# Transposed loads of k and v, the shift convolution on TensorE, and full-size first-stage tiles in an FFT convolution plus MLP kernel

## The chip, the cores and the metric

The kernel runs on one core of one Trainium2 chip. The metric is the device time of one execution in microseconds (us), the median of the fast runs. The kernel before takes 297.48 us (296.56 to 298.64, 4 runs). The profile's span is about 2 us shorter than that time: the span of the profiled run is 295.0 us.

Engines: PE is TensorE (PEld its weight loads), DVE is VectorE, ACT is ScalarE, POOL is GpSimd, SP is SyncE. Here SyncE issues every DMA, in one queue, in program order. "SPq" in the chain of waits is SyncE's own instruction stream.

## The reference

Two layers are applied twice to x, which starts as q (2048 rows of 512, bf16).

```python
# A: shift convolution, long convolution by FFT, gate
k_shift = sum over t of k_pad[:, t:t+S, :] * shift_k[:, 3 - t]     # 4 taps per channel
kv = k_shift * v
y = irfft(rfft(kv, zero padded to 2S) * rfft(ssm_k, padded)) [:S]  # long convolution
y = y + kv * ssm_D
x = x + layernorm(x) * y
# B: MLP
x = x + (gelu(layernorm(layernorm(x)) @ w1 + b1) @ w2 + b2)        # 512 -> 1376 -> 512
```

k, v, shift_k and ssm_k do not depend on x. So y is computed once, at the start, and everything after it is norms, gates and MLP blocks.

## The kernel before

A small list scheduler, `Prog`, takes operations with estimated durations and fixes the order on each engine. The program goes through these stages:

1. ssm_k (the filter) is loaded and transposed on TensorE, goes through a first transform stage (`stage1`) and a second (`stage2`, with a 6.3 MB table `tab_s2` that is loaded in 8 pieces). Result `R_H`.
2. k and v are loaded; VectorE makes the four taps of the shift convolution, adds them and multiplies with v (`shift_chunk`). Then `stage1`.
3. `products`: `stage2` of kv, times the filter's transform, on VectorE, in two halves.
4. Two inverse stages, then the norms of the first block.
5. Eight MLP blocks, four for each of the two passes.

The parts that the change touches:

```python
    dma(A(0, 128, R_SR, [1, 2048]), dr(A_shift_k, 0, [0, 128], [1, 2048]), 1 << 19)
    # ... two small loads of k for the rows that the taps reach back to ...
    for g in range(2):     # 64 partitions x 16 KB contiguous, 1 MB each
        dma(A(64 * g, 64, R_K + 1536, [1, 8192]), dr(A_k, 16 * g * 512, [32 * 512, 64], [1, 8192]), 1 << 20)
    for g in range(2):
        dma(A(64 * g, 64, R_V, [1, 8192]), dr(A_v, 16 * g * 512, [32 * 512, 64], [1, 8192]), 1 << 20)
    for j in range(8):     # the stage-2 table
        tload(t_s2, 64 * 384, j * 3072, R_S2 + j * 3072, 3072)
    # ... (cut)
    def shift_chunk(w):    # 7 operations of 128 x 2048 for each of 4 chunks
        # ... (cut: outputs tm)
        def tap(j, o):
            tt(o, A(0, 128, R_K + (3 - j) * 512 + w * 64, [512, 16], [256, 2], [1, 64]),
               A(0, 128, R_SJ[w] + j * 128, [0, 16], [64, 2], [1, 64]), ALU.mult, 1140.0)
        for j in range(3):
            tap(3 - j, tm[j])
        tt(tm[1], tm[0], tm[1], ALU.add, 1140.0)
        tap(0, tm[0])
        tt(tm[2], tm[1], tm[2], ALU.add, 1140.0)
        tt(tm[1], tm[2], tm[0], ALU.add, 1140.0)
        for h in range(2):
            # ... multiply with v, 128 x 1024 ...
        stage1(R_KP, ...)  # 512 matmuls in all, 64x64 weights, 128 columns; evicted by ScalarE alone
```

Of the kernel before, what the change touches and what calls it, by code (L numbers as in the profile page):

```python
# [44 lines left out]
class Prog:  # L45
# [7 lines left out]
    def __init__(self, nc):  # L53
        self.nc = nc
        self.ops = []
        self.state = {}
        self.nodes = [(-1, None)]
        self.cache = {}

# [60 lines left out]
    def op(self, eng, fn, dur, reads=(), writes=(), tile=None, dma=None, prio=0.0, nbytes=0, after=()):  # L120
# [4 lines left out]
        o.extra = prio  # L125
# [254 lines left out]
def _tables():  # L380
# [4 lines left out]
    F = np.stack([np.cos(th), -np.sin(th)], -1).reshape(64, 128)  # L385
    F = np.concatenate([F, F], 0)
# [25 lines left out]
AR = 105984  # L412


def bass_interleave_layers__ssm_conv_h3__mixer_channel_mlp__prompt_kernel(
# [3 lines left out]
    NS = 192  # L419
# [28 lines left out]
    R_ID, R_F, R_D, R_B1, R_SJ3 = place(128), place(128), place(16), place(16), place(512)  # L448
    R_S2 = place(64 * 384)
    R_1, R_2, R_3, R_4, R_5, R_6 = (place(n) for n in (16384, 16384, 17920, 16384, 8192, 5120))  # L450
# [4 lines left out]
    R_K, R_V, R_Y, R_U = R_3, R_3 + 19 * 512, R_3, R_3 + 16384  # L455
    R_GX, R_SR, R_X, R_T2 = R_4, R_4 + 12288, R_4, R_4 + 8192
    R_SJ = [R_4 + 8192 + 512 * w for w in range(3)] + [R_SJ3]
    R_KP, R_YT = R_5, R_5
    R_TMP, R_RING = R_6, R_6
    R_XT = R_S2  # L460
    R_HT = R_S2 + 4096
    R_N = R_S2 + 4096 + 2 * 5632
    M_B1, M_ST, M_MV, M_RS, M_HF = 0, 16, 16 + 96, 16 + 96 + 32, 16 + 96 + 32 + 16
# [15 lines left out]


    row = 128 + 128 + 512 + 4096
    P.op(ACT, lambda e: e.preload_act_table(AF.Gelu_apprx_tanh), 1300.0, prio=1e6)
    z = A(0, 1, R_K, [1, 1536])
    P.op(POOL, lambda e, z=z: e.memset(z, 0.0), 1300.0, writes=[z])
    tload(t_sm, row, 0, R_ID, 256)
    dma(A(0, 128, R_D, [1, 4]), dr(A_ssm_D, 0, [1, 128], [128, 4]), 1024)
    for b in range(4):
        dma(A(0, 128, R_HRAW + b * 2048, [1, 2048]), dr(A_ssm_k, b * 128 * 2048, [2048, 128], [1, 2048]), 1 << 19)
    dma(A(0, 128, R_SR, [1, 2048]), dr(A_shift_k, 0, [0, 128], [1, 2048]), 1 << 19)
    dma(A(64, 64, R_K, [1, 1536]), dr(A_k, 13 * 512, [32 * 512, 64], [1, 1536]), 3 << 16)  # L490
    dma(A(1, 63, R_K, [1, 1536]), dr(A_k, 29 * 512, [32 * 512, 63], [1, 1536]), 3 << 16)
    for g in range(2):
        dma(A(64 * g, 64, R_K + 1536, [1, 8192]), dr(A_k, 16 * g * 512, [32 * 512, 64], [1, 8192]), 1 << 20)
    for g in range(2):
        dma(A(64 * g, 64, R_V, [1, 8192]), dr(A_v, 16 * g * 512, [32 * 512, 64], [1, 8192]), 1 << 20)
# [3 lines left out]
    HP = 0.0  # L499
    EV_H = EV_X = (ACT,)  # L500
# [7 lines left out]
    for a4 in range(4):  # L508
        tl = Tile(dconv)
        for al in range(4):  # L510
            ins = []
            for b in range(4):
                for g in range(2):
                    src = A(0, 128, R_HRAW + b * 2048 + 16 * g + 4 * a4 + al, [32, 64])
                    ins.append((g, al * 512 + b * 128, src))

            def f(e, ins=ins, tl=tl):
                for g, o, src in ins:
                    r = e.transpose(QB(tl, 64 * g, 64, o, [1, 128]), src, IDN)
                return r  # L520
            P.op(PE, f, 8 * 60.0, reads=[x[2] for x in ins] + [IDN], tile=tl)
        dst = A(0, 128, R_HP + 16 * a4, [4, 4], [64, 128], [1, 4])

        def f(e, dst=dst, tl=tl):
            src = QB(tl, 0, 128, 0, [512, 4], [4, 128], [1, 4])
            if e is nc.scalar:
                return e.activation(dst, src, AF.Copy)
            return e.tensor_copy(dst, src)
        P.op((ACT, DVE), f, {ACT: 2048 * .833 + 60, DVE: 2048 * .52 + 70}, writes=[dst], tile=tl)

    def stage1(src, G, gk, gh, dg0, n, engs, prio=0.0):


        for d8 in range(dg0 // 8, (dg0 + n) // 8):
            for h in range(2):
                tl = Tile(dconv)
                ins = [(64 * g, i, A(64 * g, 64, src + (64 * h + 8 * d8 + i) * 64, [1, 64]), A(64 * g, 64, R_F, [1, 128]))
                       for i in range(8) for g in range(2)]

                def f(e, ins=ins, tl=tl):  # L540
                    for p, i, w, m in ins:
                        r = e.matmul(Q(tl, p, 64, i * 128, [1, 128]), w, m, start=True, stop=True)  # L542
                    return r
                P.op(PE, f, 16 * 45.0, reads=[x for y in ins for x in y[2:]], tile=tl, prio=prio)
                dst = A(0, 128, G + gh(h, 8 * d8), [gk, 128], [1, 8])

                def f(e, dst=dst, tl=tl):
                    src = Q(tl, 0, 128, 0, [1, 128], [128, 8])
                    if e is nc.scalar:
                        return e.activation(dst, src, AF.Copy)  # L550
                    return e.tensor_copy(dst, src)
                P.op(engs, f, {ACT: 1100.0, DVE: 1024 * 1.04 + 90}, writes=[dst], tile=tl, prio=prio)
# [19 lines left out]

    stage1(R_HP, R_GH, 128, lambda h, dg: 64 * (dg // 32) + 32 * h + dg % 32, 0, 64, EV_H, HP)
    for k4 in range(16):
        tl = stage2(R_GH, range(4 * k4, 4 * k4 + 4), 128, dconv, HP)
        dst = A(0, 128, R_H + k4 * 1024, [1, 1024])

        def f(e, dst=dst, tl=tl):
            src = Q(tl, 0, 128, 0, [1, 1024])
            if e is nc.scalar:  # L580
                return e.activation(dst, src, AF.Copy)  # L581
            return e.tensor_copy(dst, src)  # L582
        P.op((ACT, DVE), f, {ACT: 1024 * .833 + 60, DVE: 1024 * 1.04 + 70}, writes=[dst], tile=tl, prio=HP)

# [4 lines left out]
    for w in range(4):  # L589
        tt_out = A(0, 128, R_SJ[w], [128, 4], [64, 2], [1, 64])  # L590
        tt_in = A(0, 128, R_SR + 256 * w, [1, 4], [1024, 2], [4, 64])
        P.op(DVE, lambda e, o=tt_out, i=tt_in: e.tensor_copy(o, i), 600.0, reads=[tt_in], writes=[tt_out])

    def shift_chunk(w):

        tm = [A(0, 128, R_KP + w * 1024, [64, 16], [4096, 2], [1, 64])]
        tm += [A(0, 128, o, [128, 16], [64, 2], [1, 64]) for o in (R_TMP, R_TMP + 2048)]

        def tap(j, o):

            tt(o, A(0, 128, R_K + (3 - j) * 512 + w * 64, [512, 16], [256, 2], [1, 64]),
               A(0, 128, R_SJ[w] + j * 128, [0, 16], [64, 2], [1, 64]), ALU.mult, 1140.0)
        for j in range(3):
            tap(3 - j, tm[j])
        tt(tm[1], tm[0], tm[1], ALU.add, 1140.0)
        tap(0, tm[0])
        tt(tm[2], tm[1], tm[2], ALU.add, 1140.0)
        tt(tm[1], tm[2], tm[0], ALU.add, 1140.0)
        for h in range(2):
            tt(A(0, 128, R_KP + (64 * h + 16 * w) * 64, [4, 16], [64, 16], [1, 4]),  # L610
               A(0, 128, R_TMP + 64 * h, [128, 16], [4, 16], [1, 4]),
               A(0, 128, R_V + 256 * h + w * 64, [512, 16], [4, 16], [1, 4]), ALU.mult, 610.0)
        stage1(R_KP, R_GX + 8192 * (w // 2), 64, lambda h, dg: 32 * h + dg % 32, 16 * w, 16, EV_X)

    nx = [0]

    def products(hf):

        for k8 in range(8):
            tl = stage2(R_GX + 8192 * hf, range(8 * k8, 8 * k8 + 8), 64, dx)  # L620
            xo = R_RING + (nx[0] % 3) * 1024
            po = R_RING + 3072 + (nx[0] % 2) * 1024
            nx[0] += 1
            xb = A(0, 128, xo, [1, 1024])

            def f(e, xb=xb, tl=tl):
                return e.activation(xb, Q(tl, 0, 128, 0, [1, 1024]), AF.Copy)  # L627
            P.op(ACT, f, 1024 * .833 + 60, writes=[xb], tile=tl)
            ho = R_H + k8 * 2048 + 64 * hf
            x3 = A(0, 128, xo, [128, 8], [64, 2], [1, 64])  # L630
            tt(A(0, 128, po, [128, 8], [64, 2], [1, 64]), x3, A(0, 128, ho, [256, 8], [128, 2], [1, 64]), ALU.mult, 600.0)
            tt(x3, x3, A(0, 128, ho + 128, [256, 8], [-128, 2], [1, 64]), ALU.mult, 600.0)
            for ri, p in ((0, po), (1, xo)):
                tt(A(0, 128, R_Y + ri * 8192 + 8 * k8 * 64 + 32 * hf, [64, 8], [4096, 2], [1, 32]),
                   A(0, 128, p, [128, 8], [32, 2], [1, 32]), A(0, 128, p + 64, [128, 8], [32, 2], [1, 32]),
                   ALU.add if ri else ALU.subtract, 330.0)

    def inverse1(hf):

        for d4 in range(8 * hf, 8 * hf + 8):  # L640
            tl = Tile(dconv)
            ins = []
            for i in range(4):
                dg = 4 * d4 + i
                for ri in range(2):
                    ins.append((i, ri, A(0, 128, R_Y + ri * 8192 + dg, [64, 128]), A(0, 128, R_U + ri * 256, [1, 256])))
# [5 lines left out]
            P.op(PE, f, 8 * 115.0, reads=[x for y in ins for x in y[2:]], tile=tl)  # L652
            dst = A(0, 128, R_Z + 16 * d4, [256, 64], [4, 4], [1, 4])
# [206 lines left out]
```

## Time and profile before

What matters, with the stage borders read from the chain of waits and the timeline:

| stage (us) | before |
|---|---|
| start until v has landed and VectorE goes on | 35.7 |
| until the first product | 65.1 (+29.4) |
| until the first MLP matmul | 131.9 (+66.8) |
| until the end | 295.0 (+163.1) |

The span in 40 slices (7.4 us each) of the kernel before: a digit is the busy share in tenths, the last line what the DMA engines moved.

```profile
PE   0657086799899396329999999999999999999992
DVE  0135999999999998898890794874938611101131
DMA  6999997000099520003210301303003020200322
GB/s 203 297 213 213 224 414 284 2 18 6 2 224 296 197 97 2 1 5 69 51 20 2 71 0 28 46 0 63 8 2 71 18 53 2 71 0 2 71 71 71
```

The DMA engines are full in slices two to six, VectorE from the fifth to about the eighteenth, and TensorE from the nineteenth on. So three limits follow each other. The same with exact borders, from the busy times by window of the kernel before (columns: window, its length, then busy time of PE, PEld, DVE, ACT and POOL with instruction counts, granted clock, DMA share, GB/s):

```profile
0.00:35.70 35.70, 14.36 (x320) 12.81 (x320) 14.12 (x16) 14.20 (x13) 1.88 (x7) 0.95 0.94 224
35.70:65.10 29.40, 22.26 (x387) 18.98 (x388) 28.68 (x29) 22.57 (x24) 0.96 (x2) 0.83 0.51 196
65.10:131.90 66.80, 47.15 (x786) 41.95 (x785) 63.55 (x147) 46.65 (x52) 7.95 (x12) 0.87 0.33 92
131.90:295.00 163.10, 156.43 (x689) 64.32 (x702) 83.02 (x214) 59.54 (x88) 13.32 (x22) 0.98 0.17 36
```

VectorE is busy for 28.68 of the 29.4 us in which the shift convolution ends, and for 63.55 of the next 66.8. In the last stage it is TensorE, 156.43 of 163.1. The chain of waits of the kernel before (start, length, what) has the load of v as its first long piece:

```profile
7.51 28.18 DMA ar<-in_A_v_dram
35.69 4.62 DVE ar L587 x5
...
61.70 1.03 ACT ar L581
63.88 1.22 DVE ar L582
65.10 1.88 DVE ar L587 x4
```

The chain names v, but VectorE didn't stand still for it: by its timeline it had worked on k's taps without a gap since 25.4 us, and used v first at 36.7. So 35.7 is a border between stages, and no wait of the kernel before.

And the groups by shape (busy us, mean ns, idle time before them with its releaser). The 28 operations of 128x2048 are the shift convolution; of the 40 of 128x1024, 8 multiply with v and 32 are products.

```profile
L587 DVE TENSOR_TENSOR ar<-ar 128x2048 bf16<-128x2048 bf16 x28 | 32.9, 1220 | 7.3 <-DMA ar<-in_A_k_dram 7.0
L587 DVE TENSOR_TENSOR ar<-ar 128x1024 bf16<-128x1024 bf16 x40 | 25.9, 683 | 0.2
L542 PE MATMUL ps<-ar 64*64 64x128 bf16 x512 | 21.6, 241 | 17.3 <-DVE ar L587 10.9 <-ACT ar L550 3.1 <-ACT ar L527 2.8
```

### The profile page before, as it was taken

How to read it: one execution, taken by the hardware profiler on the slowest of the kernel's cores; microseconds unless marked ns; L12 is line 12 of the kernel's file. 1: busy time of each engine (PE TensorE's matmuls, PEld its weight loads, DVE VectorE, ACT ScalarE, POOL GpSimd, SP SyncE). 2: the span in 40 equal slices, each digit the busy share in tenths (PEclk: the TensorE clock that was granted, in tenths of full speed). 3: DMA queues.
4: the chain of work that ended last, by engine and by line, in shares of the span. 5: the costliest groups of instructions: out<-in, count | busy, mean ns of one | idle time of the engine just before them, and what ended most of it. 6: DMA issues, size and time to landing. Idle time of an engine off the chain costs nothing.

```text
span 295.0 us, 5161 instructions
## 1 busy us (share of the span) xinstructions
PE 240.2 (81%) x2177; PEld 138.1 (47%) x2192; DVE 189.4 (64%) x401; ACT 143.0 (48%) x176; POOL 24.1 (8%) x43
## 2 busy tenths in 40 slices
PE   0657086799899396329999999999999999999992
PEld 0655075588799284113433434434433444434440
DVE  0135999999999998898890794874938611101131
ACT  1069079598968469616327045152366321464000
POOL 2000000100010022210210110111101100000000
PEclk9999658999999879758999999999999999999997
DMA  6999997000099520003210301303003020200322
GB/s 203 297 213 213 224 414 284 2 18 6 2 224 296 197 97 2 1 5 69 51 20 2 71 0 28 46 0 63 8 2 71 18 53 2 71 0 2 71 71 71
DMA packets 22703, 25.75 MB, mean 87 GB/s; under 512 B 17722, under 2 KB 19355, under 8 KB 22170
## 3 DMA queue, kind: packets, MB, share of 16 engines
q1 hardware_dynamic: 22682, 25.44, 33.0%
q8 instruction: 17, 0.28, 0.4%
q14 instruction: 4, 0.03, 0.0%
HBM read 19.66 MB, written 2.10 MB: 74 GB/s over the span
## 4 chain that ended last, share of the span: by engine, by line
PE 51%; DVE 24%; DMA 10%; ACT 7%; SPq 2%; issue 2%; POOL 2%
PE ps L818 24%; PE ps L800 23%; DVE ar L587 16%; DMA ar<-in_A_v_dram 10%; DVE sm L729 3%; ACT ar L581 2%; SPq L470 2%; ACT ar L658 2%; DVE ar L743 2%; PE ps L650 2%; ACT ar L550 2%; ACT ar L627 1%; POOL sm L737 1%; DVE ar L582 1%; PE ps L566 1%
## 5 line engine op out<-in xcount | busy, mean ns | idle before, releaser
L805 ACT ACTIVATE ar<-ps,sm 128x512 bf16<-128x512 f32 (+1 forms) x88 | 59.5, 686 | 82.3 <-PE ps L800 59.1
L587 DVE TENSOR_TENSOR ar<-ar 128x512 bf16<-128x512 bf16 (+2 forms) x164 | 91.5, 618 | 8.9 <-DMA ar<-in_A_k_dram 7.0
L800 PE MATMUL ps<-ar 128*128 128x512 bf16 (+1 forms) x342 | 81.7, 385 | 1.6 <-ACT ar L789 1.2
L818 PE MATMUL ps<-ar 128*128 128x512 bf16 (+1 forms) x347 | 78.1, 379 | 0.8 <-DVE ar L822 0.6
L822 DVE TENSOR_TENSOR ar<-ar,ps 128x512 bf16<-128x512 bf16 x32 | 21.2, 682 | 65.5 <-PE ps L818 65.5
L800 PEld LDWEIGHTS ps<-ar 128*128 128x128 bf16 (+1 forms) x352 | 30.8, 101 | 50.8 <-ACT ar L805 21.4
L818 PEld LDWEIGHTS ps<-ar 128*128 128x128 bf16 (+1 forms) x352 | 33.6, 98 | 43.4 <-ACT ar L805 2.9
L729 DVE BATCH_NORM_STATS2 sm<-ar 128x6 f32<-128x512 bf16 x64 | 41.4, 681 | 0.1
L550 ACT ACTIVATE ar<-ps 128x1024 bf16<-128x1024 f32 x32 | 30.0, 1050 | 12.7 <-PE ps L542 12.7
L542 PE MATMUL ps<-ar 64*64 64x128 bf16 x512 | 21.6, 241 | 17.3 <-DVE ar L587 10.9
L566 PE MATMUL ps<-ar 128*128 128x128 bf16 (+1 forms) x192 | 30.0, 239 | 2.3 <-ACT ar L550 1.5
L743 DVE TENSOR_SCALAR ar<-ar,sm 128x512 bf16<-128x512 bf16 x64 | 23.2, 406 | 11.4 <-POOL sm L737 10.3
L568 PE MATMUL ps<-ar 128*128 128x64 bf16 (+1 forms) x192 | 29.2, 202 | 0.0
L567 PE MATMUL ps<-ar 128*128 128x64 bf16 (+1 forms) x192 | 29.1, 201 | 0.0
L542 PEld LDWEIGHTS ps<-ar 64*64 64x64 bf16 x512 | 17.9, 121 | 20.9 <-issue 9.1
L650 PE MATMUL ps<-ar 128*128 128x256 bf16 x128 | 17.7, 301 | 5.5 <-DVE ar L587 5.2
L566 PEld LDWEIGHTS ps<-ar 128*128 128x128 bf16 x192 | 18.7, 98 | 4.3 <-ACT ar L550 2.1
L568 PEld LDWEIGHTS ps<-ar 128*128 128x128 bf16 x192 | 18.8, 98 | 0.7
L650 PEld LDWEIGHTS ps<-ar 128*128 128x128 bf16 x128 | 15.7, 175 | 7.0 <-DVE ar L587 5.5
L567 PEld LDWEIGHTS ps<-ar 128*128 128x128 bf16 x192 | 18.8, 98 | 0.0
L627 ACT ACTIVATE ar<-ps 128x1024 bf16<-128x1024 f32 x16 | 15.9, 1043 | 3.3 <-DVE ar L587 3.1
L658 ACT ACTIVATE ar<-ps 128x1024 bf16<-128x1024 f32 x14 | 13.7, 1042 | 7.9 <-PE ps L650 7.9
(27 smaller groups left out, 97.0 us busy)
## 6 DMA issues: line engine op xcount, KB each, us to landing
ar<-tab_s SPq DMA_DIRECT2D x8, 768.0 KB, 34.1
ar<-in_A_ssm_k_dram SPq DMA_DIRECT2D x4, 512.0 KB, 5.5
ar<-in_A_k_dram SPq DMA_DIRECT2D x2, 1024.0 KB, 16.3
ar<-in_A_v_dram SPq DMA_DIRECT2D x2, 1024.0 KB, 25.9
ar<-in_A_q_dram SPq DMA_DIRECT2D x2, 1024.0 KB, 10.5
out_dram<-ar SPq DMA_DIRECT2D x8, 256.0 KB, 3.1
ar<-in_B_w_dram SPq DMA_DIRECT2D x1, 1376.0 KB, 8.5
ar<-in_B_w_dram SPq DMA_DIRECT2D x1, 1280.0 KB, 6.1
```

The lines of the kernel that those rows point to most:

```text
L542: r = e.matmul(Q(tl, p, 64, i * 128, [1, 128]), w, m, start=True, stop=True)
L550: return e.activation(dst, src, AF.Copy)
L566: e.matmul(Q(tl, 0, 128, i * 2 * n, [1, 2 * n]), t[0], gg[0], start=True, stop=False)
L567: e.matmul(Q(tl, 0, 128, i * 2 * n, [1, n]), t[1], gg[1], start=False, stop=False)
L568: r = e.matmul(Q(tl, 0, 128, i * 2 * n + n, [1, n]), t[2], gg[2], start=False, stop=True)
L587: return P.op(eng, lambda e: e.tensor_tensor(o, a, b, op), dur, reads=[a, b], writes=[o])
L650: r = e.matmul(Q(tl, 0, 128, i * 256, [1, 256]), w, m, start=ri == 0, stop=ri == 1)
L729: P.op(DVE, lambda e, st=st, x=x: e.bn_stats(st, x), 600.0, reads=[x], writes=[st])
L743: P.op(DVE, lambda e: e.tensor_scalar(o, x, m, r, ALU.subtract, ALU.mult), 260.0, reads=[x, m, r], writes=[o])
L800: r = e.matmul(Q(tl, 0, rows, 0, [1, 512]), w, m, start=dk == 0, stop=dk == 3)
L805: P.op(ACT, lambda e, dst=dst, tl=tl, rows=rows, bias=bias: e.activation(dst, Q(tl, 0, rows, 0, [1, 512]), AF.Gelu_apprx_tanh, bias=bias), ...
L818: r = e.matmul(Q(tl, 0, 128, 0, [1, 512]), ins[fc][0], ins[fc][1], start=fc == 0, stop=fc == 10)
```

## The change

The intent is to take the shift convolution off VectorE, which is the limit between 36 and 132 us, and give it to TensorE, which has time there. A convolution along rows, per channel, becomes a matmul with a diagonal weight matrix once channels lie on partitions: four taps are four matmuls with the data shifted by one column, summed in PSUM. For that k and v must arrive transposed, which the DMA can do (the kernel before has 28 such transposes of 128 KB inside SBUF, which held SyncE 1.27 us each, the median); and kv must be transposed back (four more DMA transposes, inside SBUF). The first transform stage then works on full 128x128 weights (128 matmuls of 256 columns for 512 of 128), its evictions are shared by ScalarE and VectorE, and the products are 2048 wide instead of 1024. Further on, the residual operations are merged to 2048 and a scheduling priority (`BIAS`) holds back the MLP blocks' operations in the scheduler's order.

```diff
-    for g in range(2):
-        dma(A(64 * g, 64, R_K + 1536, [1, 8192]), dr(A_k, 16 * g * 512, [32 * 512, 64], [1, 8192]), 1 << 20)
-    for g in range(2):
-        dma(A(64 * g, 64, R_V, [1, 8192]), dr(A_v, 16 * g * 512, [32 * 512, 64], [1, 8192]), 1 << 20)
+    for b in (0, 2, 1, 3):          # 4 transposes of 2048 rows x 128 channels, 512 KB
+        dmat(A(0, 128, R_KT + b * 2064 + 16, [1, 2048]), dr(A_k, 128 * b, [512, 2048], [1, 128]), 1 << 19)
+    for a in range(32):             # 32 transposes of 64 rows (32 apart) x 512 channels, 64 KB
+        dmat(A(0, 128, R_VT + 64 * a, [2048, 4], [1, 64]), dr(A_v, 512 * a, [32 * 512, 64], [1, 512]), 1 << 16)
     for j in range(8):
         tload(t_s2, 64 * 384, j * 3072, R_S2 + j * 3072, 3072)
@@ shift_chunk is replaced by kv(q), for the halves q = 0, 1 @@
+                    ins = [(A(0, 128, R_DG + (4 * b + j) * 128, [1, 128]),
+                            A(0, 128, R_KT + b * 2064 + 16 + 1024 * u + 512 * n - j, [1, 512])) for j in range(4)]
+                    def f(e, ins=ins, tl=tl, n=n):
+                        for j, (w, m) in enumerate(ins):
+                            r = e.matmul(Q(tl, 0, 128, 512 * n, [1, 512]), w, m, start=j == 0, stop=j == 3)
+                        return r
+                o = A(0, 128, R_KVT + 8192 * q + 64 * h + 32 * u, [128, 32], [1, 32])
+                v = A(0, 128, R_VT + 2048 * b + 32 * u, [64, 32], [1, 32])
+                P.op(DVE, lambda e, o=o, v=v, tl=tl: e.tensor_tensor(o, Q(tl, 0, 128, 0, [1, 32], [32, 32]), v, ALU.mult),
+                     1225.0, reads=[v], writes=[o], tile=tl, prio=KP[q])
+        for i in range(2):          # kv back, SBUF to SBUF, 512 KB each
+            dmat(A(0, 128, R_KP + 4096 * q + 2048 * i, [128, 16], [1, 128]), A(0, 128, R_KVT + 8192 * q + 2048 * i, [1, 2048]), 1 << 19, ...)
+        stage1(R_KP + 4096 * q, R_GX + 8192 * q, 64, EV_X, XP[q])
@@ stage 1: full tiles, and evictions by either engine @@
-    EV_H = EV_X = (ACT,)
+    EV_H = EV_X = (ACT, DVE)
@@ products: 16 x 128 instead of 8 x 128 columns in one operation @@
-            x3 = A(0, 128, xo, [128, 8], [64, 2], [1, 64])
+            x3 = A(0, 128, xo, [128, 16], [64, 2], [1, 64])
@@ (cut: tables, memory map, residuals, BIAS) @@
```

## The prediction

> **What bounds the kernel now.** The span (295.0 us) has two parts. From 131.9 us, the first MLP matmul (timeline), TensorE is the limit: windows show some 88 matmuls per 19.4 us at 97-99% busy until 289, then a 6 us tail. Little in the change shortens this. The 132 us before it are a chain: the load of v lands at 35.7 us (chain of waits: "DMA ar<-in_A_v_dram", 28 us), then VectorE is the limit (98-100% busy in the 10 us windows from 30 to 110): shift taps (28 of 128x2048 at 1220 ns, 33 us), v multiplies and products (40 at 683 ns). Products begin at 65.1 and end about 102.6; inverse, last stage and block 0 of the norm chain take until 131.9.
>
> **What the change removes and adds.**
> - VectorE loses the 28 shift operations (33 us) and 8 v multiplies (5.5 us), and gains 8 PSUM multiplies of 1024 (1.22 us each, like the casts from PSUM: 10 us), and some first-stage evictions (13 at 1.22 us, 16 us). TensorE, idle there today, gains 64 matmuls of 512 columns and swaps 512 small ones for 128 wide.
> - 2048-wide products save about 150 ns per merged pair (2x683 against 1220): 3 to 5 us.
> - k and v cross the transposing DMA in 4 + 32 instructions, and the product kv four more times 512 KB inside SBUF. The MLP's transposes show the cost: 256-byte packets of 18 ns, so 16/18 ns x 256 B = 227 GB/s, and SyncE is held 1.27 us for each 128 KB.[...] At 227 GB/s, k and v (4.2 MB) take 18.5 us, against about 21 now (16 KB packets, 180-246 GB/s), so v lands at 28-30 us instead of 35.7, provided that issuing from HBM doesn't cost SyncE time by size.[...] If it scales like the SBUF ones, v lands at 48 us.
> - The 6.3 MB stage-2 table queues behind v: lands at about 45 us (50 today). The kv transposes queue behind it: each 512 KB would hold SyncE about 4 us (estimate, by size), so first stage of half 0 starts at 48-50, where v alone would allow 36.
>
> **On the critical path.** VectorE's order: 4 kv multiplies (30-35), 6 evictions for the filter (-42), 4 kv multiplies (-47), 4 evictions after the transposes (49-54), products from about 55 (65 now). From there my sum of VectorE's queue at the durations above: 41 us to the end of products (filter evictions are mixed in), 15 us inverse and norm statistics, 13 us block 0: MLP at about 124 instead of 131.9. Most of the 38 us taken from VectorE is lost to waiting on DMA and to evictions.
>
> **Prediction:** 287 us, 274 to 304. Faster by over 2%: 0.65; within 2%: 0.18; slower: 0.17.
>
> **Shows it right:** first MLP matmul near 124; v landing near 29; first product near 55; VectorE idle before the kv multiplies and before the half-0 evictions, released by DMA; MLP part still about 162 us.
>
> **Would make it wrong:** HBM transposes issue-bound on SyncE (v at 48, products at 73, total near 305); or they run faster than 227 GB/s, or VectorE's mixed queue hides the wait, and MLP starts before 115 (total 275).

The sum is 29 + 26 + 69 + 163 us, the terms of the table below.

## The result, and the profile after

The changed kernel takes 329.63 us (329.15 to 330.33, 4 runs), against 297.48 us. The ratio is 1.108, with a 95% interval of 1.103 to 1.113: it is slower by 11%. (A ratio here is the mean time of one kernel's fast runs over that of the other's of the same rounds, so it isn't quite the ratio of the medians.) The output is correct.

| stage (us) | before | predicted | after | after less before |
|---|---|---|---|---|
| start until v has landed | 35.7 | 28 to 30 | 61.4 | +25.7 |
| v to first product | 29.4 | 26 | 31.6 | +2.2 |
| first product to first MLP matmul | 66.8 | 69 | 70.3 | +3.5 |
| MLP to the end | 163.1 | 163 | 164.3 | +1.2 |
| span | 295.0 | 287 | 327.6 | +32.6 |

The slices of the changed kernel, 8.2 us each:

```profile
PE   0890000399799884595399699999999999999993
DVE  0320000595667999898985875878877678401102
DMA  6972222699900946500000330020303032320202
GB/s 210 224 124 49 48 56 48 201 422 253 190 5 2 211 132 225 166 2 2 0 0 2 64 65 0 13 54 0 66 0 64 0 75 57 70 60 0 64 2 64
```

From the fourth to the seventh slice TensorE and VectorE do nothing, and the DMA engines, for whose data they wait, are at 20% and move about 50 GB/s, where the first two slices show over 200. Somebody is not giving the DMA engines work. By stages:

```profile
0.00:61.40 61.40, 14.68 (x158) 10.46 (x160) 5.21 (x13) 5.02 (x8) 0.76 (x7) 0.73 0.46 105
61.40:93.00 31.60, 27.60 (x257) 20.57 (x259) 22.06 (x20) 18.57 (x19) 0.48 (x3) 0.93 0.96 271
93.00:163.30 70.30, 49.49 (x755) 44.69 (x754) 64.33 (x93) 41.88 (x45) 4.87 (x8) 0.89 0.31 86
163.30:327.60 164.30, 155.51 (x689) 70.42 (x702) 97.08 (x199) 60.47 (x88) 15.64 (x26) 0.97 0.17 36
```

The granted clock of 0.73 in the first stage is a mean: it is 1.00 from 10 to 22 us, where TensorE is busy for 10.17 of 12 us, and 0.50 from 30 to 61, where it runs nothing. So the clock isn't what makes this stage long. Note also the third line: VectorE is busy 64.33 us between the first product and the first MLP matmul, against 63.55 before. The change did not relieve VectorE in this stage: in the groups of this window the SBUF operations (products and gates) fall from 39.0 to 32.5 us and the statistics of the norms from 14.2 to 9.4, as some move behind the border, but the evictions from PSUM grow from 8.4 to 19.3. What the change took off VectorE lies in the first two lines, 27.3 us together for 42.8, and there VectorE is not the limit any more.

The chain of waits of the changed kernel tells who was slow:

```profile
4.64 5.52 SPq L486
10.21 2.62 SPq L486
12.87 2.98 SPq L486
15.89 2.94 SPq L486
18.86 1.25 SPq L486
20.16 1.25 SPq L486
21.45 1.25 SPq L486
...
57.60 1.25 SPq L486
58.89 2.49 DMA ar<-in_A_v_dram
61.40 2.37 DVE ar L621 x2
...
79.46 4.37 DMA ar<-ar
83.88 1.97 PE ps L546 x16
```

L486 is the helper that issues a DMA transpose. The first four entries are k's (512 KB each), and then come 32 equal entries of 1.25 us, v's (64 KB each). One every 1.29 us, 32 of them are 41.3 us, from 18.86 to 60.14. Each piece lands 2.5 us after its issue begins, as the list of DMA issues says:

```profile
ar<-in_A_v_dram SPq DMA_TRANSPOSE x32, 2.5
```

so the data aren't what is late; the issue is. What waits for it, by shape:

```profile
L621 DVE TENSOR_TENSOR ar<-ps,ar 128x1024 bf16<-128x1024 f32 x8 | 9.2, 1215 | 44.8 <-DMA ar<-in_A_v_dram 41.3 <-PE ps L616 3.5
L546 PE MATMUL ps<-ar 128*128 128x256 bf16 x128 | 18.4, 293 | 41.6 <-DVE ar L621 38.3 <-DMA ar<-ar 2.5 <-ACT ar L554 0.5
L592 DVE TENSOR_TENSOR ar<-ar 128x2048 bf16<-128x2048 bf16 x30 | 36.0, 1220 | 3.1 <-ACT ar L638 2.5
```

The multiply with v (L621) has 44.8 us of idle time before it where the shift convolution before had 7.3. TensorE's 41.6 us before L546 are mostly the same wait once removed (38.3 of them): the filter's first stage stands behind the kv matmuls, whose PSUM is not free until L621 has run.

A second thing shows in SyncE's issue times (start, end, length in us), listed from the trace:

```
58.89 60.14  1.25  transpose, v, the last of 32
60.19 64.35        table, 8 loads of 768 KB, 0.43 to 0.64 each
66.05 79.42 13.37  transpose, kv, first
79.46 82.48  3.03  transpose, kv, second
83.16 85.18  2.02  transpose, kv, third
85.22 87.74  2.52  transpose, kv, fourth
```

The first kv transpose holds SyncE for 13.4 us and the others for 2 to 3. It was issued just after 6.3 MB of table, and its hold ends at 79.42, when the last piece of the table has landed (79.31, by the trace). How much of this wait reaches the products is another question: TensorE had other work until 81.42 and stood idle for the transposes only 2.5 us, the "<-DMA ar<-ar 2.5" in the line of L546 above.

### The profile page after: what moved, and what is told of

The parts are those of the page before. It is cut to its first block, busy times and chain, and to the rows that moved or that the text cites. A ratio compares the mean times of both kernels' runs of the same rounds, so it can differ in the third digit from the quotient of the medians.

```text
span 327.6 us, 4461 instructions
## 1 busy us (share of the span) xinstructions
PE 247.3 (75%) x1854; PEld 146.1 (45%) x1872; DVE 188.7 (58%) x323; ACT 125.9 (38%) x160; POOL 21.8 (7%) x44
## 4 chain that ended last, share of the span: by engine, by line
PE 62%; SPq 18%; DVE 12%; DMA 3%; ACT 2%; issue 2%; POOL 0%
PE ps L812 24%; PE ps L830 23%; SPq L486 16%; DVE ar L592 6%; PE ps L546 4%; PE ps L661 3%; PE ps L570 3%; DMA ar<-ar 2%; PE ps L616 1%; ACT ar L586 1%; PE ps L572 1%; PE ps L571 1%; DVE sm L741 1%; DVE ar L621 1%; DVE ar L555 1%
## 5 line engine op out<-in xcount | busy, mean ns | idle before, releaser
L817 ACT ACTIVATE ar<-ps,sm 128x512 bf16<-128x512 f32 (+1 forms) x88 | 60.5, 687 | 90.6 <-PE ps L812 90.6
L812 PE MATMUL ps<-ar 128*128 128x512 bf16 (+1 forms) x345 | 80.8, 393 | 4.5 <-DMA ar<-ar 3.0
L830 PE MATMUL ps<-ar 128*128 128x512 bf16 (+1 forms) x344 | 77.0, 379 | 0.4
L812 PEld LDWEIGHTS ps<-ar 128*128 128x128 bf16 (+1 forms) x352 | 36.2, 103 | 48.2 <-issue 5.8
L830 PEld LDWEIGHTS ps<-ar 128*128 128x128 bf16 (+1 forms) x352 | 34.4, 98 | 41.5
L592 DVE TENSOR_TENSOR ar<-ar 128x2048 bf16<-128x2048 bf16 (+1 forms) x50 | 48.1, 1004 | 3.1 <-ACT ar L638 2.5
L546 PE MATMUL ps<-ar 128*128 128x256 bf16 x128 | 18.4, 293 | 41.6 <-DVE ar L621 38.3
L741 DVE BATCH_NORM_STATS2 sm<-ar 128x6 f32<-128x512 bf16 x64 | 43.8, 691 | 1.5
L554 ACT ACTIVATE ar<-ps 128x1024 bf16<-128x1024 f32 x19 | 18.6, 1029 | 46.8 <-PE ps L546 46.4
L621 DVE TENSOR_TENSOR ar<-ps,ar 128x1024 bf16<-128x1024 f32 x8 | 9.2, 1215 | 44.8 <-DMA ar<-in_A_v_dram 41.3
L546 PEld LDWEIGHTS ps<-ar 128*128 128x128 bf16 x128 | 14.3, 148 | 45.7 <-DVE ar L621 39.3
L661 PE MATMUL ps<-ar 128*128 128x256 bf16 x128 | 15.8, 288 | 8.0 <-ACT ar L669 8.0
L570 PEld LDWEIGHTS ps<-ar 128*128 128x128 bf16 x192 | 18.8, 98 | 3.5 <-ACT ar L586 1.6
L572 PEld LDWEIGHTS ps<-ar 128*128 128x128 bf16 x192 | 18.8, 98 | 0.7
L571 PEld LDWEIGHTS ps<-ar 128*128 128x128 bf16 x192 | 18.8, 98 | 0.1
L661 PEld LDWEIGHTS ps<-ar 128*128 128x128 bf16 x128 | 14.9, 173 | 8.7 <-ACT ar L669 8.2
L555 DVE CAST ar<-ps 128x1024 bf16<-128x1024 f32 x13 | 15.1, 1218 | 3.4 <-PE ps L546 3.4
```

Of the source, the lines that this page charges most:

```text
L546: r = e.matmul(Q(tl, 0, 128, i * 256, [1, 256]), w, fb, start=True, stop=True)
L570: e.matmul(Q(tl, 0, 128, i * 2 * n, [1, 2 * n]), t[0], gg[0], start=True, stop=False)
L571: e.matmul(Q(tl, 0, 128, i * 2 * n, [1, n]), t[1], gg[1], start=False, stop=False)
L572: r = e.matmul(Q(tl, 0, 128, i * 2 * n + n, [1, n]), t[2], gg[2], start=False, stop=True)
L592: return P.op(eng, lambda e: e.tensor_tensor(o, a, b, op), dur, reads=[a, b], writes=[o])
L661: r = e.matmul(Q(tl, 0, 128, i * 256, [1, 256]), w, m, start=ri == 0, stop=ri == 1)
```

## The experiments

Three theories stood at the start. First (T1): a DMA transpose from HBM holds SyncE for some 1.25 us whatever its size, so 32 of them cost 41 us. Its rival: v's pieces are slow because their 64 rows lie 32 rows apart in HBM, a matter of the data. Second (the "second wait"): the long kv transpose waits in SyncE's queue behind the table. Third: the priority and the order of the filter's stage cost something of their own.

All runs gave correct results. Each batch was compared with runs of the kernel before on the same chip (296.28, 296.94, 296.69 and 296.62 us in the four batches).

### v_four: v in four transposes

```diff
-    for a in range(32):
-        dmat(A(0, 128, R_VT + 64 * a, [2048, 4], [1, 64]), dr(A_v, 512 * a, [32 * 512, 64], [1, 512]), 1 << 16)
+    for b in (0, 2, 1, 3):
+        dmat(A(0, 128, R_VT + b * 2048, [1, 2048]), dr(A_v, 128 * b, [512, 2048], [1, 128]), 1 << 19)
-                v = A(0, 128, R_VT + 2048 * b + 32 * u, [64, 32], [1, 32])
+                v = A(0, 128, R_VT + 2048 * b + 1024 * u, [1, 32], [32, 32])
```

> The edit: v in 4 transposes of 2048 rows x 128 columns (512 KB each, as k), in natural column order, the multiply reads v with a stride of 32 instead. Theory T1 (each HBM transpose holds SyncE about 1.25 us whatever its size, so 32 of them take 41 us; the data alone needs 2.6 to 3.0 us per 512 KB, as k's show): v's four take about 12 us, v lands at about 33 us (61.4 in the changed kernel), products begin near 62 (93), first MLP matmul near 133 (163), time about 300 us. Rival T2 (the cost goes by the bytes or by the 64x128 pieces, 0.31 us each, not by the instruction): v still lands near 60, time about 330 us. Rival T3 (the load of v does not set the pace, the queue of VectorE and the kv transposes do): v lands early, but the time falls by less than 10 us, above 319.

Measured: 299.90 us, ratio to before 1.014 (1.011 to 1.017). That is what T1 expected. The median is 29.7 us under the changed kernel's (of another batch), of the 32 us that were lost. SyncE held 2.2 to 2.7 us for each of v's four transposes, and the first multiply ran at 24.3 us. The rows are now in natural order, so the multiply reads v with a stride of 32 elements, and that has a price:

```profile
L621 DVE TENSOR_TENSOR ar<-ps,ar 128x1024 bf16<-128x1024 f32 x8 | 14.6, 1876 | 6.6 <-PE ps L616 3.5 <-DMA ar<-in_A_v_dram 3.1
```

1876 ns against 1215. Yet the first product comes at 64.2 us, hardly before the 65.1 of the kernel before. The time that v now arrives early is lost again. The first kv transpose held SyncE 14.4 us, from 33.98 to 48.41, behind the table (its last piece landed at 48.31). But TensorE stood idle for it only 3.1 us, up to 52.9: before that it had the filter's first stage to do, which stood behind the kv matmuls once more, and half 1's kv matmuls.

### v_sizes: the same rows in pieces of four sizes

```diff
+    for b, n in ((0, 1), (2, 4), (1, 8), (3, 16)):
+        m = 2048 // n
+        for j in range(n):
+            dmat(A(0, 128, R_VT + b * 2048 + j * m, [1, m]), dr(A_v, 128 * b + 512 * m * j, [512, m], [1, 128]), 256 * m)
```

> A measurement of the disputed cost: v's four column blocks in 1, 4, 8 and 16 transposes (512, 128, 64 and 32 KB each), natural order. T1: SyncE is held 2.6 to 3.0 us for 512 KB[...], and about 1.25 us for each of 128, 64 and 32 KB alike. T2 (by bytes): about 2.9, 0.72, 0.36 and 0.18 us. If by 64x128 piece (0.31 us): 128 KB (8 pieces) 2.5 us, 64 KB 1.25 us, 32 KB 0.62 us. v lands near 57 us under T1.

What counts is SyncE's hold per instruction, from the trace:

| size | instructions | hold of each, us |
|---|---|---|
| 512 KB | 1 | 2.40 |
| 128 KB | 4 | 1.26 |
| 64 KB | 8 | 1.24 (1.25 for the scattered rows of the changed kernel) |
| 32 KB | 16 | 1.23 |

(One of 32 KB took 2.07 and is left out.) Between 32 and 128 KB the hold does not depend on the size, and contiguous rows cost what scattered ones do. Only the one of 512 KB took longer. v landed at 58.0, and T1 expected 57.

### v_rows: four transposes with the layout of the changed kernel

Eight neighbouring rows make one row of 4096 elements, so four transposes of 64 rows of 4096 give the same order within v as the 32 small ones, with the same step of 32 KB between the rows in HBM.

```diff
-    for a in range(32):
-        dmat(A(0, 128, R_VT + 64 * a, [2048, 4], [1, 64]), dr(A_v, 512 * a, [32 * 512, 64], [1, 512]), 1 << 16)
+    for a in range(0, 32, 8):
+        dmat(A(0, 128, R_VT + 256 * a, [64, 32], [1, 64]), dr(A_v, 512 * a, [32 * 512, 64], [1, 4096]), 1 << 19)
@@ (cut: the multiply reads v at this layout's places) @@
```

> The edit: v again in 4 transposes of 512 KB, but of 64 rows x 4096 contiguous elements, which put v into just the layout of the 32 small ones, so that the multiply keeps its 1.22 us (1.85 in v_four). T1 (per-instruction hold of SyncE): v lands near 31 us as in v_four, the time is that of v_four or up to 3 us less, 296 to 300 us, against 330 for the changed kernel. Rival (what made v slow was the gather of rows 32 KB apart, not the number of instructions): v lands near 60 and the time is near 330.

Measured: 299.67 us, ratio 1.011 (1.007 to 1.015). The chain of waits and the multiply of this kernel:

```profile
26.21 4.51 DMA ar<-in_A_v_dram
30.75 2.37 DVE ar L621 x2
...
L621 DVE TENSOR_TENSOR ar<-ps,ar 128x1024 bf16<-128x1024 f32 x8 | 9.2, 1217 | 13.2 <-DMA ar<-in_A_v_dram 9.6 <-PE ps L616 3.5
```

v is there at 30.75 instead of 61.4, and the multiply is back at 1217 ns. The same order at an eighth of the instructions is 30 us faster: T1 holds, and the rival of scattered rows falls. The first product is at 65.3, once more where it was before the change, since the first kv transpose again held SyncE (13.0 us, 35.39 to 48.38). The stages of v_rows are 30.75, +34.6, +70.8 and +162.9 us.

### table_first, v_four_tf: is the kv transpose waiting behind the table?

Both issue the table before v; v_four_tf also before k, with v in four pieces as in v_four.

```diff
@@ table_first: the eight table loads moved ahead of v's 32 transposes
@@ v_four_tf: ahead of k's and v's four transposes each
```

> The edit: only the order of issue, the 6.3 MB stage-2 table before v's 32 transposes. T1 plus a second wait (the first kv transpose holds SyncE 13.4 us at 66 us[...]): v lands about 3.6 us later (65), but the first kv transposes take about 3 us each instead of 13.4, half-0 evictions begin near 76 (84.6), products near 85 (93); time about 321 us. Rival (the 13.4 us are the kv transpose's own cost by size): half-0 evictions near 88, time about 333 us.

Measured: 339.09 us, ratio 1.145 (1.139 to 1.150). A miss, in the wrong direction. The first two kv transposes now held SyncE 1.8 and 2.8 us instead of 13.4 and 3.0, so the 13.4 us were a wait behind the table. But v came at 71.1, 9.7 us later: issuing the table took SyncE 4.7 us first, and three of v's transposes held it 2.8 to 3.3 us behind the table. (The small transposes did not hold it until the table was through, as the 512 KB one had: by 37.0 us, when the table's last piece landed, six were issued.) And the first product came at 102.2, 31.1 us after v, where the changed kernel has 31.6. So taking this wait away gained next to nothing by itself: the transposes had landed at 82.5, but TensorE was busy without a gap with the filter's first stage and half 1's kv matmuls until it came to half 0's first stage at 89.1.

> The edit: both, v in 4 transposes, and the order table, k, v. T1: table lands near 25, k near 36, v near 48, the filter's path is done meanwhile[...]; half-0 evictions near 57, products near 61, fewer filter evictions among them, first MLP matmul near 125 to 130, time 290 to 295 us, less than v_four. If only v's landing counts (no second wait), it is slower than v_four by about 10 us.

Measured: 301.72 us, ratio 1.021 (1.016 to 1.027). Missed by 6.7 us or more. Now k's first transpose stood behind the table and held SyncE 17.9 us (8.71 to 26.63); the last multiply ended at 55.4 and the first product came at 65.5. v's last transpose landed at 48.0, 17 us later than in v_four, and the first product only 1.3 us later. The long wait moved from one 512 KB transpose to another, the first behind the table each time.

### v_four_actq, v_four_actq_ff: the table in ScalarE's queue

```diff
-        tload(t_s2, 64 * 384, j * 3072, R_S2 + j * 3072, 3072)
+        tload(t_s2, 64 * 384, j * 3072, R_S2 + j * 3072, 3072, ACT, [last])   # issued by ScalarE, after v
@@ both also: k's and v's bytes doubled in the scheduler's estimates @@
@@ v_four_actq_ff also: the kv matmuls wait for the filter's first stage (after=filt)
```

The aim of v_four_actq is that the kv transposes no longer stand behind the table in SyncE's queue, where the first of them was held 14.4 us in v_four.

> The edit, on v_four: the stage-2 table is issued from ScalarE's queue, after the last v transpose has landed (and the scheduler is told twice the bytes for k and v, near their measured time)[...]. Theory (second wait: in v_four the first kv transpose holds SyncE 14.4 us[...]): the first two kv transposes take 2 to 3 us each (sharing the engines with the table), half-0 evictions from about 48 to 51 instead of 54.9, products near 57 instead of 64, time 290 to 294 us against 300. Rival (the table's own landing, which stage 2 needs too, is the limit[...]): products within 2 us of v_four, time 298 to 301.

Measured: two fast runs, 297.23 and 298.27 us, and two slow ones of 306.3 that are left out; ratio of fast runs 1.002 (0.994 to 1.010). Missed. The kv transposes came through (1.35 and 3.52 us), but VectorE then stood idle for 5.1 us, up to 60.0, for TensorE, which ran second-stage matmuls from 52.5 to 60.0 without a gap, and products began at 61.3, 2.9 us earlier than in v_four.

> The edit, on v_four_actq: the kv matmuls wait for the filter's first-stage evictions. Theory (in the changed kernel the four kv tiles take all eight PSUM banks as soon as k is there and hold them until v lands, and the filter's first stage waits for a bank, though its data has been there since 20 us): the filter's first stage ends by about 30 us, its second stage runs while the table lands, products begin near 50 with few filter evictions among them, first MLP matmul near 113 to 118, time 279 to 285 us, below before. Rival (VectorE's total work sets the time, its order doesn't): within 1.5% of v_four_actq.

(The eight banks are the program's: its scheduler gives out the PSUM tensor, 128x4096 in f32, in eight parts, and a kv tile of 1024 columns takes two.)

Measured: 295.58 us, ratio 0.994 (0.988 to 1.000). Missed by over 10 us. The table now moves while the kv transposes do, in another queue, and the first two kv transposes held SyncE 11.7 and 5.4 us. Products began at 67.0, but not for that alone: the second of them had landed at 57.2, while the order on TensorE put all of the filter's second stage first, without a gap from 45.5 to 58.3. In the trace of the changed kernel a transpose's packets are of 256 bytes (18 ns each) and the table's of 6144 (234 ns). How the DMA engines divide their time between two queues no run shows, so why the transposes were slow beside the table stays open. Here a separate queue did not rescue the transposes that met the table.

### v_four_wr: natural reads, strided writes

The same as v_four with the strided access on the output side (256 bytes from element to element) instead of v's (64 bytes) and PSUM's (128 bytes, in the changed kernel too).

```diff
-                o = A(0, 128, R_KVT + 8192 * q + 64 * h + 32 * u, [128, 32], [1, 32])
+                o = A(0, 128, R_KVT + 8192 * q + 64 * h + 32 * u, [1, 32], [128, 32])
-                v = A(0, 128, R_VT + 2048 * b + 1024 * u, [1, 32], [32, 32])
+                v = A(0, 128, R_VT + 2048 * b + 1024 * u, [32, 32], [1, 32])
@@ and PSUM is read as [32, 32], [1, 32] instead of [1, 32], [32, 32] @@
```

> The edit, on v_four: the kv multiply runs in natural column order, so that PSUM and v are read in order and the result is written with a stride of 256 bytes, where v_four reads v with a stride of 64 bytes and the multiply takes 1.85 us instead of 1.22. If the strided 2-byte read of v is what costs, it is back at 1.22 us; if any large stride costs, it stays near 1.85. The time changes by at most 1.5% either way[...].

Measured: 318.31 us, ratio 1.070 (1.064 to 1.077). Missed: the multiply became 2.6 times as long as in v_four, four times as long as in the changed kernel.

```profile
L621 DVE TENSOR_TENSOR ar<-ps,ar 128x1024 bf16<-128x1024 f32 x8 | 36.8, 4883 | 6.4 <-PE ps L616 3.3 <-DMA ar<-in_A_v_dram 3.1
```

So the stride has its price in SBUF: 1215 ns with runs of 32 neighbours in v and in the output (the changed kernel), 1876 with a 64-byte stride in v (v_four), 4883 with a 256-byte stride in the output alone (this run). The 128-byte steps through PSUM show no price: with them the multiply takes the 1215 ns of the changed kernel, where a plain copy from PSUM of this size takes 1218. Whether it is the side or the size of the stride that makes 4883 of 1876, no run tells apart.

### v_four_narrow: 1024-wide products

```diff
@@ v_four, with each 2048-wide product operation split in two of 1024, and each sum of 1024 in two of 512
```

> The edit, on v_four: products and sums in 1024 and 512 columns again, as before the change, everything else left. The merged operations are worth about 150 ns per pair: 16 pairs of products and 16 pairs of sums, so 3 to 5 us slower than v_four (303 to 305), if VectorE is the limit during the products, as its 95 to 100% busy windows say; within 1 us of v_four if it isn't.

Measured: 300.14 us, ratio 1.010 (1.004 to 1.015), against 1.014 of v_four in another batch. Missed: wide products gain nothing here that shows in the time. A pair of narrow ones costs 150 ns more (2 x 685 against 1223), but the narrow ones start earlier (61.5 against 64.2 us), because the first need not wait for two PSUM tiles, and end at 103.1 against 103.8. VectorE did 3.6 us more work in that stretch (40.4 against 36.9), and it fitted in.

### after_ff and after_nobias: order and priority in the changed kernel

```diff
@@ after_ff: the kv matmuls wait for the filter's first stage (after=filt)
@@ after_nobias
-BIAS = 19000.0
+BIAS = 0.0
```

> The edit, on the changed kernel, v's 32 transposes left: the kv matmuls wait for the filter's first-stage evictions, so that they can't hold all PSUM banks until v is there. Theory (PSUM held from 23 to 61 us while v is loaded): the filter's first stage is done by 30 us; after v (61) VectorE has only multiplies, half 1 is multiplied by 71 instead of 82;[...] fewer evictions before the first product, first MLP matmul 3 to 6 us earlier, time 323 to 327 us against 330. Rival (PSUM isn't what stops the filter): no change.

Measured: 330.81 us, ratio 1.116 (1.113 to 1.119); no gain, and the theory that held-up PSUM by itself costs time falls. The filter's first stage was done by 26 us, and the second half's multiplies ended at 74 instead of 82, but half 0 still waited for the transpose behind the table. TensorE now stood idle for it for 10.2 us, up to 82.8, where the changed kernel has 2.5. So the two waits hid each other: this run takes the one away, table_first the other, and neither alone brings the products nearer to v (33.1 and 31.1 us after it, 31.6 in the changed kernel).

> The edit, on the changed kernel: the priority penalty of later MLP blocks (BIAS) set to 0. The MLP part was 164.3 us from its first matmul to the end, against 163.1 before, with 2.9 us of waiting for block 1's transposes, though the penalty was meant to order it better. If the penalty costs: the MLP part falls to 162 or less, time down 1 to 3 us. If it helps: first MLP matmul later by 1 us or more, time up. If it is of no weight: within 1 us of the changed kernel (329.6).

Measured: 329.43 us, ratio 1.109 (1.103 to 1.115). The priority has no weight for the time, but for the reason that two effects cancel: without it the first MLP matmul comes 6.3 us later (169.6) and the MLP part takes 158.3 us instead of 164.3. Both the sign of a cost and the sign of a help that the expectation names were there.

### before_4k: the kernel before with k and v in 4 KB rows

A side question: k's and v's 16 KB packets in the kernel before moved only about 200 GB/s (201 and 202 by window, from 13.0 to 25.4 and from there to 35.7 us), where ssm_k's 4 KB ones moved some 412 (159 ns each, on 16 engines). Is it the size of the packet?

```diff
-        dma(A(64 * g, 64, R_V, [1, 8192]), dr(A_v, 16 * g * 512, [32 * 512, 64], [1, 8192]), 1 << 20)
+        for j in range(0, 8192, 2048):      # and k in the same way
+            dma(A(64 * g, 64, R_V + j, [1, 2048]), dr(A_v, 16 * g * 512 + j, [32 * 512, 64], [1, 2048]), 1 << 18)
```

> The edit, on the kernel before: k and v loaded plainly in 4 KB rows (16 DMAs of 256 KB) instead of 16 KB rows (4 DMAs of 1 MB), nothing transposed. The trace of before shows 16 KB packets at about 205 GB/s over 16 engines and 4 KB packets at about 410. If the packet size is the cause, v lands near 24 us instead of 35.7, the shift starts near 17 instead of 25, and the time falls by 7 to 11 us, to 286 to 290. If the 64-partition destination is the cause, v lands within 2 us of before and the time is unchanged.

Measured: 296.77 us, ratio 0.999 (0.996 to 1.003). Packets of 4096 bytes took 322 ns (median) in these loads, 159 ns in ssm_k's. It isn't the size. The two loads differ in the number of partitions (64 against 128) and in the step between rows (32 KB against 4 KB); no run here tells which of them it is.

### q0_first: keep the table out of the transposes' way

v_rows, with the loads of k for half 0 first, the kv matmuls after the filter's first stage, and the table, with the filter's second stage, after half 0's two kv transposes. The ground for it: the first kv transpose was held 14.4 us with the table ahead of it in the same queue (v_four) and 11.7 with the table in another (v_four_actq_ff).

```diff
+    loadk(0); loadk(2)          # then v in four transposes, then loadk(1); loadk(3)
+    last = kv(0)                # multiplies and the two kv transposes of half 0
+    for j in range(8):
+        tload(t_s2, 64 * 384, j * 3072, R_S2 + j * 3072, 3072, [last])
@@ the filter's second stage moved here @@
+    kv(1)
```

> The edit, on v_rows: order of loads k0 k2 v k1 k3; the table is issued after the first two kv transposes instead of before; the kv matmuls wait for the filter's first-stage evictions. Theory[...]: kv transposes of half 0 take 2 to 3 us each at 30 to 36, half-0 evictions from about 37 (54.9 in v_four), products begin near 44 to 48 (64), first MLP matmul near 115, time 276 to 283 us, faster than before by over 4%. Rival (the DMA's total bytes, or the table's landing, limit the front part in any order): products not before 55, time 290 or more.

Measured: 290.40 us, ratio 0.979 (0.975 to 0.982): faster than the kernel before by 2.1% (1.8 to 2.5, so whether by over 2% isn't settled), but 7 us short of what was expected; the time and the start of the products are those that the rival named. The kv transposes of half 0 held SyncE 1.8 and 2.7 us and its evictions began at 44.4, 10 us earlier than in v_four. The products began at 56.2, 9.1 us earlier than in v_rows. Several things changed at once here, and their shares weren't measured. The filter's first stage in front alone (after_ff) gained nothing, and the table out of the way without it (v_four_actq) 2.9 us. Before the products VectorE then stood idle, from 49.9 to 55.0, as its timeline shows (the bracket is the idle time before the entry):

```profile
48.66 1.22 DVE L679 CAST ar<-ps 128x1024 bf16<-128x1024 f32 x1
54.97 1.22 DVE L679 CAST ar<-ps 128x1024 bf16<-128x1024 f32 x1 [5.08 <-PE ps L577]
56.23 1.23 DVE L586 TENSOR_TENSOR ar<-ar 128x2048 bf16<-128x2048 bf16 x1
```

L577 is the second stage, which needs the table. But TensorE was not waiting for a piece of it in that time. It ran second-stage matmuls without a gap, as its window shows (PE busy in all of the 7.35 us):

```profile
47.58:54.93 7.35, 7.35 (x146) 6.99 (x143) 2.21 (x2) 4.97 (x6) 0.00 (x0) 1.00 1.02 421
```

So VectorE waited for TensorE's queue. The late table bears on this in another way: its first piece landed at 44.9, so none of the filter's second stage had been done before half 0's first stage; in q0_split below, 24 of its matmuls ran at 40.1 to 42.0. And half 1's first transpose holds SyncE 14.4 us behind the table.

### q0_split: three pieces of the table before, five after

```diff
@@ q0_first, with table pieces 0 to 2 issued before kv(0) and 3 to 7 after it
```

> The edit, on q0_first: three of the table's eight pieces are issued before the first kv transposes, where the DMA engines stood idle from 30 to 35.5 us, five after them as before. Theory (after the loads, the front part is bound by the DMA's bytes and by these idle 6 us; in q0_first the products waited for table pieces until 56): table complete near 52 instead of 58, products begin near 51 (56), first MLP matmul near 121 (126), time 284 to 287 us against 290.4. If VectorE's queue is the limit from there on, less than 2 us is gained.

Measured: 289.95 us, ratio 0.978 (0.973 to 0.982), 0.45 us under q0_first's median in another batch, no difference that can be told from noise; the expected 284 to 287 was missed. Products began 3.4 us earlier, at 52.86 (the timeline), and the first MLP matmul came at 124.47, only 1.7 us earlier than q0_first's 126.18. The stage between, by window:

```profile
52.86:124.47 71.61, 50.79 (x756) 45.46 (x754) 64.39 (x93) 41.94 (x45) 5.43 (x11) 0.88 0.44 106
```

VectorE is busy for 64.39 us of it: the same 64 us as in the changed kernel, and about what it was before. So VectorE's own queue is the likely floor of this stage, and earlier data could only help by what it takes off the other 7 us. No run takes work off VectorE there to test it. With q0_first this is the fastest version tried, about 2.2% (1.8 to 2.7) under the kernel before. No fuller step was tried.

## Why the prediction was wrong

The prediction was 287 us with a range of 274 to 304; it came to 329.6. The sum was 29 + 26 + 69 + 163; it turned out 61.4 + 31.6 + 70.3 + 164.3.

**The step that failed is the first term**: "so v lands at 28-30 us instead of 35.7, provided that issuing from HBM doesn't cost SyncE time by size". The condition was the wrong question. Issuing does cost SyncE time, but by the instruction: 1.25 us each, and 1.23 to 1.26 us from 32 to 128 KB alike (v_sizes). 32 of them are 41 us, and v landed at 61.4, off by 32 us: this one term is most of the 42.6 us of the miss. The named risk, "issue-bound on SyncE (v at 48, products at 73, total near 305)", was the right place with the wrong law: it scaled the 1.27 us that the trace shows for each 128 KB transpose by size, which gives 32 such units for k and v together. In that trace all transposes have the same size, so it couldn't tell a cost per byte from a cost per instruction. 32 instructions for v alone cost those 41 us, with k's on top; and 41 us were never set against the 9 us of v's bytes (half of the 18.5 us for k and v). v_four and v_rows, which change only how many instructions bring v, take 30 us back.

The size of the pieces shows in the rate: those of just 64 KB ran at 50 GB/s, and k's of 512 KB, after the first, at 176 to 200 (524,288 bytes in 2.98 and 2.62 us of SyncE's time).

**The second term, v to products, was 26 and is 31.6.** That it came so near is partly luck. The mechanism was in the prediction ("The kv transposes queue behind it: each 512 KB would hold SyncE about 4 us"), but its size was wrong: the first kv transpose held 13.4 us. And the result, first stage 19 to 21 us after v, was nearly right at 22.5 (83.9 less 61.4) for another reason too: TensorE had other work until 81.4, so the transpose cost it only the 2.5 us up to 83.9. In table_first, where the transposes hardly held SyncE, the first product came 31.1 us after v all the same. From the last stage-1 eviction to the first product, 89.2 to 93.0, it took another 3.8 us, where VectorE waits 2.5 us for the first ScalarE copies (the releaser in the group of L592); the prediction had 1 us.

**The third and fourth terms were right** (70.3 for 69, 164.3 for 163), though the border between them hangs on the scheduler's priority: without it (after_nobias) it lies 6.3 us later, at the same total. "Most of the 38 us taken from VectorE is lost to waiting on DMA and to evictions" holds: between the first product and the MLP VectorE is as busy as before, and over the whole span it is busy 188.7 us for 189.4. "2048-wide products save [...] 3 to 5 us" did not show in the time (v_four_narrow). The last 2 us of the miss are an oversight: the sum is a span, and the time is 2 us above the span.

**What was there to gain** is shown by q0_split. With 4 transposes for v's 32, the filter's first stage in front, and half 0's kv transposes ahead of most of the table, the products start 12 us earlier than before (52.86 for 65.1), and 7 us of that remain at the end, since the stage after it is 4.8 us longer (71.61 for 66.8), with VectorE busy for 64 us of it in both. The intent, relief for VectorE, is met only in the shift convolution's own stage.

What stays open: the last stage of the changed kernel is 1.2 us longer, where its trace shows TensorE idle for 4.5 us before the first MLP layer's matmuls (1.6 before), 3.0 of them for a DMA transpose inside SBUF; in after_nobias this wait is gone and the last stage is 158.3 us, but the stage before it is longer by as much. Open too is how the gain of q0_first divides among its changes, and why the 64-partition loads of the kernel before (201 and 202 GB/s) are half as fast as the 128-partition ones (some 412).

## What to carry to other kernels

Cost a DMA transpose by the instruction as well as by the byte, and take the larger: at 1.25 us of the issuing engine each (measured from 32 to 128 KB), pieces under about 256 KB are bound by issue (an estimate: 1.25 us at the 200 GB/s that k's large pieces reached). When DMA engines are at 20% while everyone waits for a load, look at the queue of the engine that issues, not at the bytes. And do not issue megabytes of big packets just ahead of a large transpose that somebody waits for: here its issuer stood still for 13.0 to 14.4 us (v_rows, the changed kernel, v_four), until about when they had landed (79.42 and 79.31 us in the changed kernel, 48.41 and 48.31 in v_four). But look at what the waiting engine would do in the meantime before you count on a gain: the wait behind the table and TensorE's own queue hid each other, and only the runs that changed both started the products 9 to 12 us earlier than in v_rows.

## What was measured of the DMA and of VectorE

- A transpose from HBM held SyncE 1.23 to 1.26 us for 32, 64 and 128 KB alike (v_sizes; plain loads in the changed kernel: mostly 0.43 to 0.67 us).
- k's 512 KB transposes from HBM, after the first, took 2.6 to 3.0 us of SyncE's time, 176 to 200 GB/s (the changed kernel), and v's in v_four landed 2.0 to 2.4 us apart, some 230 GB/s; their 256-byte packets of 18 ns make 227 GB/s over 16 engines. Plain loads with packets of 4 and 6 KB (159 and 234 ns, the changed kernel) make 412 and 420.
- A 512 KB transpose issued behind or beside a large plain load held its issuing engine: 13.0 us (v_rows), 13.4 (the changed kernel) and 14.4 (v_four) for an SBUF transpose behind a 6.3 MB table in the same queue and 17.9 for one from HBM (v_four_tf), and 11.7 beside it in another queue (v_four_actq_ff), against 1.8 and 2.8 in table_first and 1.8 and 2.7 in q0_first, where the table was not in the way. Of the 64 KB ones behind it in table_first none was held over 3.3 us.
- A 128x1024 multiply of a PSUM tile with a bf16 tile took 1215 ns (the changed kernel), 1876 with a 64-byte stride in the bf16 input (v_four), and 4883 with a 256-byte stride in the output (v_four_wr).
